# Positions instead of channels on the partitions for theta, and seven quadrant products for both pairs of batches

## The chip, the cores and the metric

One core of one Trainium2 chip. The metric is the device time of the whole program, in microseconds (us), the median of several runs.

## The reference, cut to what matters

Three layers follow each other, on four batches of 448 positions: attention (12 heads of 64), a gated MLP with spatial mixing ("moe"), and the layer that the change rewrites ("moe2"), in float32:

```python
def _moe2_ref(x, w_theta, w_tok_r, w_tok_i, w_ch):      # x: (4, 448, 768)
    theta = x @ w_theta                                  # w_theta: (768, 768)
    zr, zi = x * np.cos(theta), x * np.sin(theta)
    yr = np.einsum('ts,bsd->btd', w_tok_r, zr)           # w_tok_r, w_tok_i: (448, 448)
    yi = np.einsum('ts,bsd->btd', w_tok_i, zi)
    u = x + yr + yi
    return (u + np.maximum(u @ w_ch, 0.0)).astype(np.float32)   # w_ch: (768, 768)
```

Most weights arrive as 64-bit floats and are turned into 32-bit words on the chip.

## The kernel before, in words

**Precision.** A product of two float32 matrices is made of three matmuls in fp32r: both factors are split into a rounded part h and the rest l = x - h, and `three` gives h.h + h.l + l.h (L407). A split is one copy on ACT (h) and one subtraction on DVE or POOL (l, `difference`, L404).

**Layout.** From the first MoE on, an activation is held turned: `x2(b, m)` is a tile with 128 of the 768 channels on the partitions and the 448 positions in the columns; KD = 6 such blocks m for each of B = 4 batches b.

**The order of the work.** The program is a list of operations (`Plan.op`, L245): an engine, a due time, a cost, a function that issues the instructions, and keys that it reads and writes. The due times and costs don't run anything any more: `ORDER` (L47 to L217) is a permutation of all operations, written out as a list, and the instructions are issued in exactly that order, each engine's own in the order in which they stand there. Keys such as ("mm", 0) are buffers that are used in turn (`ring`).

**Theta and the mix (L1540 to L1676).** For each batch `split_x` (L1554) splits its six blocks. For each of the 24 blocks (b, m), `theta` (L1567) makes theta for 128 channels by 448 positions: 6 x 3 matmuls with the weights as the stationary factor and x as the moving one, 448 columns, into a bank "mm" (`th_ps`). Then come, on 448 columns each: `turns` on DVE (L1584, n = theta/2pi rounded by a magic number), `whole` on POOL (L1587), `rest_1`, `rest_2` and `clamp` on DVE (L1591 to L1599), in `second` `size` on DVE (L1603), `cosine` and `sine` on ACT (L1608 to L1612), and `real` and `imaginary` on DVE (L1616 to L1621), which multiply by x2. The result z (cos part and sin part side by side, 896 columns) has channels on the partitions. `mix` (L1633) needs positions there, since it sums over them: seven PE transposes of 128 x 128 turn z into a bank "s" (`z_ps`, L1651), ACT rounds all 896 columns (L1656), DVE subtracts (L1661, counted at L405), and 7 x 3 matmuls of 448 columns with the turned weights w_tok (`tok`) give y (`y_ps`), which DVE adds to x2 in place (L1673). The mix of a block stands two blocks behind its theta.

**Mixing weights.** `load_tok` (L1446) loads w_tok_r and w_tok_i, converts them, and `transpose_tok` (L1485) turns them in 7 steps kk of four PE transposes each (`tok_ps`, L1496), split into `tok_h` and `tok_l`.

**w_ch.** `load_w_ch` (L1682) loads it in 12 pieces of 128 x 384, converts and splits each at once into `ch_h` and `ch_l` (L405).

**Last product.** Batches 0 and 1 are done directly (L1713 to L1769): for each block 6 x 3 matmuls of 448 columns (`f_ps`), relu and sum on DVE, four PE transposes back (`o_ps`, L1751), copies and stores. Batches 2 and 3 are done together by `pair` (L1953): w_ch in four quadrants A11 to A22 and the two batches as a matrix of 2 x 2 blocks B, Winograd's form with seven products P1 to P7 in place of eight. Each product is 3 rows by 3 steps by 3 matmuls of 448 columns. `make_s` (L1859) makes the four sums S1 to S4 of quadrants, `begin` and `go_on` the sums T1 to T4 of the blocks of B, all of them split again; `plus` (L2026) adds products up in the parts `p`, `finish` (L2031) ends a block. The S parts lie in buffers of w_theta, the B parts in those of `tok` and of x's splits, the parts `p` and temporaries in those of z, zt and r.

Of the kernel before, what the change touches and what calls it, by code (L numbers as in the profile page):

```python
# [340 lines left out]
def attn_moe_moe2_kernel(ctx: ExitStack, tc: tile.TileContext, q, k, v, cap, w_in, w_sp, b_sp, w_out,  # L341
# [86 lines left out]
    def bank(over=True):  # L428
        turn[0] += over
        tag = ("mm", "av", "mm", "sum")[turn[0] % 4] if over else "mm"  # L430
        if tag == "mm":
            return ring("mm", 2), lambda: ps_mm.tile([128, 512], F32, tag="mm", name="ps_mm")
        return tag, lambda: ps_1.tile([128, 512], F32, tag=tag, name="ps_" + tag)

    def from_f64(t, bits, bits_key, hb, hb_key, wf, wf_key, to=None, to_key=None, early=1e9, engine="act"):


        n = {}
# [1339 lines left out]

# [423 lines left out]
```

## Time and profile before

| | |
|---|---|
| median of 3 runs (range) | 769.49 us (768.89 to 770.06) |
| the profiled execution: time / span | 769.43 us / 767.4 us |
| PE matmul / weight load busy | 752.9 us (98%) / 644.6 us (84%) |
| DVE / ACT / POOL busy | 603.4 (79%) / 453.3 (59%) / 300.0 us (39%) |
| instructions | 10971, of them 3732 matmuls |
| DMA | 59.26 MB, mean 77 GB/s |

The engines are PE (TensorE matmuls), PEld (its weight loads, which overlap), DVE (VectorE), ACT (ScalarE), POOL (GpSimd) and SP (which issues DMAs). A group's line of the profile gives the code line, the engine, the operation, output <- inputs by the program's names, the shape, the count, then busy us and the mean ns of one, then the idle time before them and what ended it. Matmuls overlap, so the mean of one is longer than the distance between two.

### The profile page before, as it was taken

Reading aid. Unit: us, or ns where it says so; the run is one execution under the profiler, and the core shown is the slowest. Engines: PE = TensorE matmul, PEld = TensorE weight load, DVE = VectorE, ACT = ScalarE, POOL = GpSimd, SP = SyncE. Lnnn points to the kernel's source line nnn. Section 1 sums busy time; section 2 is a strip of 40 time slices with the busy share of each in tenths; the row PEclk is TensorE's granted clock in tenths of the full one; section 3 lists DMA queues with packets and bytes.
Section 4 is the critical chain, followed back from the end, with each engine's and each line's share of the span. In section 5 each row is a group of like instructions: output and inputs, shape, how many; then the busy total and the mean of one; then the engine's idle time right before and its main releaser. Section 6 shows DMA issues by size and latency. Waiting matters only on the chain.

```text
span 767.4 us, 10971 instructions
## 1 busy us (share of the span) xinstructions
PE 752.9 (98%) x3732; PEld 644.6 (84%) x3732; DVE 603.4 (79%) x984; ACT 453.3 (59%) x752; POOL 300.0 (39%) x441
## 2 busy tenths in 40 slices
PE   8999899999999999999999999999999999999997
PEld 4665678888898888887899988999999999999986
DVE  4878978799677989889977766887778878757575
ACT  4999868787788788895565544423433333242333
POOL 4889587555445546651202001200201201437270
PEclk9999999999999999999999999999999999999999
DMA  6778333262333431412443410011010100000225
GB/s 175 202 195 211 79 86 95 60 132 56 79 98 71 117 87 42 119 37 61 125 145 102 144 46 1 21 30 33 21 42 21 41 21 1 2 1 0 73 77 139
DMA packets 78219, 59.26 MB, mean 77 GB/s; under 512 B 47074, under 2 KB 71364, under 8 KB 78164
## 3 DMA queue, kind: packets, MB, share of 16 engines
q1 hardware_dynamic: 76260, 54.61, 27.2%
q0 software_dynamic: 1152, 3.64, 1.5%
q8 instruction: 29, 0.48, 0.3%
q10 hardware_dynamic: 752, 0.33, 0.2%
q14 instruction: 26, 0.21, 0.1%
HBM read 44.18 MB, written 5.62 MB: 65 GB/s over the span
## 4 chain that ended last, share of the span: by engine, by line
PE 86%; DVE 5%; ACT 4%; POOL 2%; issue 2%; SPq 1%; DMA 0%; DVEq 0%; POOLq 0%; ACTq 0%
PE ps_mm L402 19%; PE y_ps L402 14%; PE acc L402 12%; PE th_ps L402 11%; PE f_ps L402 10%; PE sc L402 8%; PE ps_av L402 3%; PE ps_sum L402 3%; PE z_ps L1651 2%; PE tqk L709 2%; ACT e L819 1%; ACT e L822 1%; PE o_ps L1751 1%; DVE ll L405 1%; SPq L615 1%
## 5 line engine op out<-in xcount | busy, mean ns | idle before, releaser
L402 PE MATMUL y_ps<-tok_h,zt 128*128 128x448 f32 x336 | 104.6, 368 | 0.0
L1587 POOL TENSOR_SCALAR n<-n 128x448 f32<-128x448 f32 x24 | 15.0, 623 | 184.0 <-DVE n L1584 179.5
L822 ACT ACTIVATE e<-e,cap_sb 128x896 f32<-128x896 f32 x72 | 74.7, 1044 | 0.8
L819 ACT ACTIVATE e<-sc,icap 128x896 f32<-128x896 f32 x72 | 71.8, 1004 | 3.1 <-PE sc L402 2.3
L405 DVE TENSOR_TENSOR ll<-e,hh 128x896 fp32r<-128x896 f32 x54 | 62.8, 1167 | 8.3 <-ACT hh L827 4.8
L402 PEld LDWEIGHTS y_ps<-tok_h,zt 128*128 128x128 f32 x336 | 63.2, 188 | 6.1
L402 PE MATMUL y_ps<-tok_l,zt 128*128 128x448 f32 x168 | 62.0, 369 | 0.0
L1656 ACT CAST zt<-z_ps 128x896 fp32r<-128x896 f32 x24 | 21.8, 907 | 66.5 <-PE z_ps L1651 61.5
L402 PE MATMUL f_ps<-x,ch_h 128*128 128x448 f32 (+2 forms) x204 | 57.9, 365 | 0.7 <-DVE p L2028 0.5
L402 PE MATMUL th_ps<-x,th_ah 128*128 128x448 f32 x192 | 56.0, 373 | 0.2 <-DVE r L1591 0.2
L402 PE MATMUL ps_mm<-w_in_h,x 128*128 128x512 f32 (+1 forms) x132 | 47.4, 399 | 1.1 <-DVE w_sp_l L405 1.1
L402 PE MATMUL ps_mm<-x,w_in_h 128*128 128x448 f32 x168 | 48.4, 369 | 0.0
L405 POOL TENSOR_TENSOR x<-x,x 128x448 fp32r<-128x448 f32 x18 | 22.9, 1278 | 64.6 <-ACT x L1557 64.6
L402 PE MATMUL sc<-yl,XH 128*128 128x448 f32 x126 | 46.0, 365 | 0.0
L402 PE MATMUL acc<-ll,vh 128*128 128x448 f32 x108 | 40.4, 374 | 1.3 <-DVE ll L405 1.2
L405 DVE TENSOR_TENSOR zt<-z_ps,zt 128x896 fp32r<-128x896 f32 x24 | 26.2, 1091 | 18.9 <-ACT zt L1656 18.5
L402 PEld LDWEIGHTS f_ps<-x,ch_h 128*128 128x128 f32 x204 | 37.2, 188 | 4.4 <-DVE p L2028 0.9
L402 PE MATMUL acc<-hh,vh 128*128 128x448 f32 x108 | 39.5, 366 | 0.2 <-ACT xun L909 0.2
L402 PE MATMUL acc<-hh,vl 128*64 128x448 f32 x108 | 39.6, 367 | 0.0
L402 PEld LDWEIGHTS th_ps<-x,th_ah 128*128 128x128 f32 x192 | 35.0, 188 | 3.2 <-DVE r L1591 0.4
L402 PE MATMUL f_ps<-x,ch_l 128*128 128x448 f32 (+2 forms) x102 | 36.9, 362 | 0.0
L846 POOL TENSOR_SCALAR et_hl<-et 64x448 fp32r<-64x448 f32 x36 | 23.7, 658 | 32.3 <-ACT et L822 11.1
(306 smaller groups left out, 2244.4 us busy)
## 6 DMA issues: line engine op xcount, KB each, us to landing
y<-y SPq DMA_DIRECT2D x60, 112.0 KB, 2.3
bits<-in_moe_w_ch_dram SPq DMA_DIRECT2D x12, 384.0 KB, 3.1
rq<-in_q_dram SPq DMA_DIRECT2D x33, 128.0 KB, 3.1
rk<-in_k_dram SPq DMA_DIRECT2D x11, 384.0 KB, 4.2
r<-d SPq DMA_DIRECT2D x16, 224.0 KB, 3.8
rv<-in_v_dram SPq DMA_DIRECT2D x18, 192.0 KB, 2.7
w_in_bits<-in_moe_w_in_dram POOLq DMA_DIRECT2D x6, 512.0 KB, 5.3
w_in_bits<-in_moe_w_in_dram SPq DMA_DIRECT2D x6, 512.0 KB, 5.1
```

The lines of the kernel that those rows point to most:

```text
L402: nc.tensor.matmul(out=ps, lhsT=a, rhs=r, start=(first and i == 0), stop=(last and i == len(terms) - 1))
L405: (engine or nc.vector).tensor_tensor(out=o, in0=x, in1=f32(hi), op=ALU.subtract)
L615: queue.dma_start(out=twice()[0][hd][:, :, u], in_=q[b, h + hd, 0:384, :].rearrange("(r j) d -> r j d", j=3))
L709: nc.tensor.transpose(o, a, ident)
L819: nc.scalar.activation(out=st["e", g], in_=src, func=ACTF.Tanh, scale=icap)
L822: nc.scalar.activation(out=st["e", g], in_=st["e", g], func=ACTF.Exp, scale=cap_sb)
L846: nc.gpsimd.tensor_scalar(out=st["t", hd][r, :], in0=st["e", 0][r, :], scalar1=1.0, scalar2=0.0, op0=ALU.mult, op1=ALU.add)
L1587: nc.gpsimd.tensor_scalar(out=st["n"], in0=st["n"], scalar1=1.0, scalar2=-MAGIC, op0=ALU.mult, op1=ALU.add)
L1651: nc.tensor.transpose(st["t"][:, kk * 128:(kk + 1) * 128], z["z"][:, kk * 128:(kk + 1) * 128], ident)
L1656: nc.scalar.copy(out=st["h"].rearrange("p c n -> p (c n)"), in_=st["t"][:, 0:n])
L1751: nc.tensor.transpose(st["t"][0:w, i * 128:(i + 1) * 128], x2(b, m)[:, i * 128:i * 128 + w], ident)
```

## The change

Theta is made with positions on the partitions. Two batches' last 64 positions are put together into one tile of 128 (`split_tails`, tag xT), so a pair of batches has seven tiles of positions: four go with the even batch (three full ones and the shared tail), three with the odd one. The channels go in three units of 256. A unit has two halves d of 512 columns (two tiles of positions, or one in the odd batch's second half). x is the stationary factor, w_theta the moving one, with 256 columns. z comes out as the mix wants it, and is not turned; instead x is turned (fp32, into a bank "s", 10 or 6 transposes per unit), and `real` and `imaginary` multiply by it there. For the shared tail, cos and sin parts of one batch are placed on the two halves of the partitions, so `tok` gets an eighth step kk, with the two halves of w_tok exchanged. The first half of z is split by POOL, the second by DVE.

w_ch is converted but not split when it is loaded. Its quadrants are split before the first pair (`split_a`), into buffers of the tails, of the loads, of z and of zt; `make_s` adds whole numbers instead of h and l parts. `pair` runs for both pairs; the direct product is gone. `ORDER` is new throughout (3433 operations instead of 3395).

```diff
@@ transpose_tok
-        for kk in range(NC):
+        for kk in range(NC + 1):
             transpose_tok(t + 22.0 + 1.2 * kk, kk, slots)
...
-                nc.tensor.transpose(st["ps"][:, j * 128:j * 128 + n], ta[j // 2][0:n, j % 2, kk * 128:(kk + 1) * 128],
-                                    ident[0:n, 0:n])
+                if kk < NC:
+                    nc.tensor.transpose(o, a[:, kk * 128:(kk + 1) * 128], ident[0:n, 0:n])
+                    continue
+                nc.tensor.transpose(o, a[:, S - 128:S], ident[0:n, 0:n])
+                nc.tensor.transpose(o[LO], a[:, S:S + 64], ident[0:n, 0:n])
@@ split_tails (new): per batch of the pair
+        op("none", t - 1.0, 0.0, begin, r=["region"], w=[("xT", x, n) for x in "hl" for n in range(2)])
...
+            op("act", t, 0.5, lambda b=b: hi(b), r=rows, w=[("xT", "h", n)])
+            op("dve", t + 0.6, 0.5, lambda b=b: lo(b), r=rows + [("xT", "h", n)], w=[("xT", "l", n)], port=True)
@@ theta
-        t = chain(t, km, begin, [
-            (3 * C, lambda i=i: three(theta_w("h", i, m), theta_w("l", i, m), xs["h", i], xs["l", i]),
...
+        tiles = ((0, 1), (2, 3)) if even else ((0, 1), (2,))
...
+                    for k, m in enumerate(ms):
+                        o = st["x"][:, d * 512 + j * TW + k * 128:][:, 0:128]
+                        if p < 3:
+                            nc.tensor.transpose(o, x2(b, m)[:, p * 128:p * 128 + 128], ident)
+                        else:
+                            nc.tensor.transpose(o, x2(b + 1, m)[:, S - 128:S], ident)
+                            nc.tensor.transpose(o[LO], x2(b, m)[:, M:S], ident)
...
+                        for k in range(i, i + 2):
+                            xh, xl = positions(p, k)
+                            products(sd["ps"][:, j * TW:(j + 1) * TW], three(xh, xl, weights("h", k), weights("l", k)),
+                                     k == 0, k == KD - 1)
...
+            def hi(sd=sd, d=d, zd=zd, spans=spans):
+                st["H", d] = pools["wk"].tile([128, 4, TW], F32R, tag="H", name="zt", bufs=3)
...
+            e = "pool" if d == 0 else "dve"
...
+                ("act", 5.5, 0.9, hi, dict(r=[zr, zi, "region"], w=[zh])),
+                (e, 6.5, 2.1 if e == "pool" else 0.9, lambda lo=lo, e=e: lo(e=nc.gpsimd if e == "pool" else nc.vector),
+                 dict(r=[zr, zi, zh, "region"], w=[zl], port=True))] + [
+                ("act", 7.0, 0.35, tail_hi, dict(r=[zr, zi, "region"], w=[kth])),
+                ("dve", 7.4, 0.34, tail_lo, dict(r=[zr, zi, kth], w=[ktl], port=True))] * tail))
@@ mix
-                nc.tensor.transpose(st["t"][:, kk * 128:(kk + 1) * 128], z["z"][:, kk * 128:(kk + 1) * 128], ident)
...
-        op("pe", t, 0.77, transposes, r=z["zk"], w=[ks])
-        op("act", t + 0.9, 0.8, hi, r=[ks], w=["zth", "ztl"])
-        op("dve", t + 1.8, 1.0, lo, r=[ks, "zth"], w=["ztl"])
...
+            (3 * C, lambda i=i: three(z("H", i)[:, cols], z("L", i)[:, cols], tok["h", i // 4][:, i % 4, :],
+                                      tok["l", i // 4][:, i % 4, :]), keys(i) + [("tok", "h", i), ("tok", "l", i)])
+            for i in (0, 1, 4, 5, 2, 6, 3 if b % 2 == 0 else 7)])
@@ the loop over units: theta of unit i, mix of unit i - 1, then the split of unit i's second half
+    for i in range(B * N3 + 1):
...
+        if i >= 1:
+            b, c, z, keys = units[i - 1][:4]
+            for m in (2 * c, 2 * c + 1):
+                t = mix(b, m, z, keys, ("av", "sum")[n % 2], t)
...
+        if i < B * N3:
+            units[i][4]()
@@ the direct product of batches 0 and 1
-    for b in range(B - 2):
-        xs = split_x(b, t - 3.0)
...
-                (3 * C, lambda i=i, cols=cols, xs=xs: three(ch["h", i // 2][:, i % 2, cols], ch["l"][:, i, cols],
-                                                            xs["h", i], xs["l", i]),
...
@@ the quadrants' homes, their split, and make_s
+    HOMES = [("xT", None, 4), ("bits", None, 2), ("z", zs[0][1], 2), ("z", zs[1][1], 2), ("H", 0, 2)]
...
+    def split_a(q, i, t, e):
...
+        op("act", t, 0.42, lambda: nc.scalar.copy(out=a_of(q, i, "h"), in_=f32(w_of(q, i))), r=[kw], w=[kh])
+        op(e, t + 0.5, 0.47 if e == "dve" else 0.95, lambda: difference(
...
-        add(t, lambda: part(A21, "h"), lambda: part(A22, "h"), P, [key(A21, "h"), key(A22, "h")])
-        add(t + 0.1, a, lambda: part(A21, "l"), P, [kf, key(A21, "l")])
-        add(t + 0.2, a, lambda: part(A22, "l"), P, [kf, key(A22, "l")])
+        add(t, w(A21), w(A22), P, [w_key(A21, i), w_key(A22, i)])
         split(t + 0.3, 1)
...
@@ the end
-    t = pair(B - 2, t)
+    for c0 in range(0, B, 2):
+        t = pair(c0, t)
```

## Rows read from the trace of the kernel before

**Rows 1.** The clock of the core: us from first to last instruction, mean granted clock.
```profile
core 0: 767.4 us, clock 1.000
```
**Rows 2.** The page, part 1: busy us, share of the span, instructions.
```profile
PE 752.9 (98%) x3732; PEld 644.6 (84%) x3732; DVE 603.4 (79%) x984; ACT 453.3 (59%) x752; POOL 300.0 (39%) x441
```
**Rows 3.** Stages: length; PE, PEld, DVE, ACT, POOL busy; granted clock; DMA share; GB/s.
```profile
445.00:675.00 230.00, 229.79 (x1203) 209.46 (x1203) 176.09 (x322) 82.17 (x162) 39.10 (x46) 1.00 0.08 22
675.00:740.00 65.00, 64.90 (x341) 59.43 (x339) 42.86 (x72) 23.81 (x57) 31.54 (x26) 1.00 0.13 43
740.00:767.40 27.40, 22.00 (x132) 19.05 (x130) 17.00 (x30) 8.41 (x25) 5.05 (x5) 1.00 0.38 101
```
**Rows 4.** The page, part 4: the chain that ended last, by engine.
```profile
PE 86%; DVE 5%; ACT 4%; POOL 2%; issue 2%; SPq 1%; DMA 0%; DVEq 0%; POOLq 0%; ACTq 0%
```
**Rows 5.** Timeline of PE (start, us, what): theta matmuls, 24 from first row to last.
```profile
459.45 0.57 PE L402 MATMUL th_ps<-x,th_ah 128*128 128x448 f32 x2
...
464.32 0.69 PE L1496 MATMUL tok_ps<-ident,ta 128*128 128x128 f32 x4
```
**Rows 6.** Timeline of PE, the end: three matmuls of 256 columns, three of 192.
```profile
760.41 0.39 PE L402 MATMUL f_ps<-x,ch_h 128*128 128x256 f32 x2
...
760.76 0.37 PE L402 MATMUL f_ps<-x,ch_h 128*128 128x192 f32 x2
...
762.28 0.38 PE L402 MATMUL f_ps<-x,ch_h 128*128 128x192 f32 x2
...
762.61 0.39 PE L2097 MATMUL o_ps<-ident,x 128*128 128x128 f32 x2
```
**Rows 7.** Timeline of PE: seven transposes of z, three theta matmuls, the next ones.
```profile
564.54 0.93 PE L1651 MATMUL z_ps<-ident,z 128*128 128x128 f32 x7
565.22 0.65 PE L402 MATMUL th_ps<-x,th_ah 128*128 128x448 f32 x2
...
565.91 0.57 PE L402 MATMUL th_ps<-x,th_ah 128*128 128x448 f32 x2
```
**Rows 8.** Timeline of PE: two steps of turning the mixing weights, and the next matmul.
```profile
450.34 1.37 PE L1496 MATMUL tok_ps<-ident,ta 128*128 128x128 f32 x8
451.64 0.67 PE L402 MATMUL th_ps<-x,th_ah 128*128 128x448 f32 x2
```
**Rows 9.** Groups on DVE, whole span, shapes apart.
```profile
L405 DVE TENSOR_TENSOR zt<-z_ps,zt 128x896 fp32r<-128x896 f32 x24 | 26.2, 1091 | 18.9 <-ACT zt L1656 18.5
L1584 DVE TENSOR_SCALAR n<-th_ps 128x448 f32<-128x448 f32 x24 | 14.8, 618 | 3.3 <-PE th_ps L402 3.2
L405 DVE TENSOR_TENSOR ch_l<-wf,ch_h 128x384 fp32r<-128x384 f32 x12 | 6.5, 549 | 0.0
L2082 DVE TENSOR_TENSOR p<-f_ps,p 128x256 f32<-128x256 f32 x1 | 0.4, 424 | 0.1
```
**Rows 10.** Groups on POOL (445 to 675 us) and on ACT (400 to 767 us).
```profile
L405 POOL TENSOR_TENSOR x<-x,x 128x448 fp32r<-128x448 f32 x9 | 11.1, 1238 | 18.9 <-ACT x L1557 18.9
L1656 ACT CAST zt<-z_ps 128x896 fp32r<-128x896 f32 x24 | 21.8, 907 | 66.5 <-PE z_ps L1651 61.5 <-PE y_ps L402 5.0
```
**Rows 11.** Timeline of PE where theta starts; in brackets the idle time before.
```profile
466.13 0.68 PE L402 MATMUL th_ps<-x,th_ah 128*128 128x448 f32 x2 [0.21 <-DVE r L1591]
```
**Rows 12.** Timeline of PE, 740 us to the end: waits before products.
```profile
743.54 0.68 PE L402 MATMUL f_ps<-x,ch_h 128*128 128x448 f32 x2 [0.49 <-DVE p L2028]
...
746.89 1.48 PE L402 MATMUL f_ps<-x,S 128*128 128x448 f32 x6 [0.38 <-DVE p L2028]
...
758.54 0.88 PE L402 MATMUL f_ps<-x,S 128*128 128x448 f32 x3 [0.35 <-DVE p L2028]
```
**Rows 13.** Timelines of POOL and DVE: two subtractions that overlap.
```profile
668.51 1.02 POOL L1880 TENSOR_TENSOR S<-s_f,S 128x384 fp32r<-128x384 f32 x1 [4.12 <-ACT S L1876]
668.88 1.06 DVE L1880 TENSOR_TENSOR S<-s_f,S 128x384 fp32r<-128x384 f32 x1 [0.94 <-ACT S L1876]
```
**Rows 14.** Timeline of PE's weight loads in the last product.
```profile
697.03 0.19 PEld L402 LDWEIGHTS f_ps<-x,ch_l 128*128 128x128 f32 x1
```

More of the change, by code (lines that the diff above doesn't have):

```diff
@@ L459, in sign @@
             wu, top = wf().bitcast(U32), words()[:, :, 1]
-            ends = [(wu, top, wu)]
+            ends = [(wu if out is None else out().bitcast(U32), top, wu)]
             if to is not None:
@@ new lines, in attn_moe_moe2_kernel, with theta, transposes, weights @@
+    tl = {}
+    def theta(b, c, xs, t):
+        even = b % 2 == 0
+        ks = ring("s", 2)
+        ms = (2 * c, 2 * c + 1)
+        tiles = ((0, 1), (2, 3)) if even else ((0, 1), (2,))
+        st = {}
+        kth, ktl = [("tl", c, x) for x in "hl"]
+        def transposes():
+            st["x"] = ps_s.tile([128, 1024], F32, tag="s", name="x_ps")
+            for d in range(2):
+                for j, p in enumerate(tiles[d]):
+                    for k, m in enumerate(ms):
[5 more added lines that the diff above has]
+                            nc.tensor.transpose(o[LO], x2(b, m)[:, M:S], ident)
+        def weights(x, i):
+            return th[x, i][:, c * TW:(c + 1) * TW] if c < 2 else th[x, "b", i // 2][:, i % 2, :]
+        def positions(p, i):
+            if p < 3:
+                return xs["h", i][:, p * 128:p * 128 + 128], xs["l", i][:, p * 128:p * 128 + 128]
+            return xtail["x"][:, i, 0, :], xtail["x"][:, i, 1, :]
+        later = []
+        kd = []
+        for d in range(2):
+            stage("t%d" % d, b, c)
+            w = TW * len(tiles[d])
+            km, kn = ring("mm", 2), ring("vt", 3)
@@ new lines, in theta, with turns, whole @@
+            if d == 0:
+                op("pe", t, 0.109 * (10 if even else 6), transposes,
+                   r=[("x2", a, m) for a in ((b, b + 1) if even else (b,)) for m in ms], w=[ks])
+                t += 0.109 * (10 if even else 6)
+            def turns(sd=sd, w=w):
+                sd["n"] = keep.tile([128, w], F32, tag="vt", name="n", bufs=3)
+                nc.vector.tensor_scalar(out=sd["n"], in0=sd["ps"][:, 0:w], scalar1=INV_2PI, scalar2=MAGIC, op0=ALU.mult, op1=ALU.add)
+            def whole(sd=sd):
+                nc.gpsimd.tensor_scalar(out=sd["n"], in0=sd["n"], scalar1=1.0, scalar2=-MAGIC, op0=ALU.mult, op1=ALU.add)
@@ new lines, in tail_hi, with tail_lo @@
+            def tail_hi(sd=sd):
+                tl[c] = pools["wk"].tile([128, 2, TW], F32R, tag="tl%d" % c, name="zt_tail")
+                for o, a in tail_spans(sd, tl[c][:, 0]):
+                    nc.scalar.copy(out=o, in_=a)
+            def tail_lo(sd=sd):
+                for (o, a), (h, _) in zip(tail_spans(sd, tl[c][:, 1]), tail_spans(sd, tl[c][:, 0])):
+                    difference(o, a, h)
+            wide = w / 512
+            op("dve", t + 0.2, 0.6 * wide, turns, r=[km], w=[kn])
@@ new lines, in record, with rounded @@
+        def record(d, t_, ops_):
+            for e, dt, cost, f, kw in ops_:
+                op(e, t_ + dt, cost, f, **kw)
+        stage("z0", b, c)
+        record(*later[0])
+        stage("z1", b, c)
+        record(later[1][0], later[1][1], later[1][2][:5])
+        def rounded():
+            stage("zr", b, c)
+            record(later[1][0], later[1][1], later[1][2][5:])
+        where = {0: (0, 0), 1: (0, 1), 4: (0, 2), 5: (0, 3), 2: (1, 0), 6: (1, 2)}
+        where[3 if even else 7] = (1, 1) if even else None
@@ L1643, in mix, with z, keys @@
+        def z(x, i):
+            if where[i] is None:
+                return tl[c][:, "HL".index(x)]
+            return st[x, where[i][0]][:, where[i][1]]
+        def keys(i):
+            return [kth, ktl] if where[i] is None else kd[where[i][0]]
+        return b, c, z, keys, rounded, t
+    def mix(b, m, z, keys, bank, t):
         stage("m", b, m)
         st = {}
-        ks = ring("s", 2)
-        n = NC * 128
-        def transposes():
-            st["t"] = ps_s.tile([128, 1024], F32, tag="s", name="z_ps")
-            for kk in range(NC):
-                nc.tensor.transpose(st["t"][:, kk * 128:(kk + 1) * 128], z["z"][:, kk * 128:(kk + 1) * 128], ident)
@@ L1653, in hi @@
[L1653 to L1663 removed]
+        cols = slice(m % 2 * 128, m % 2 * 128 + 128)
@@ L1690, in load_w_ch, with load, hb @@
-        converted(t, w_ch[i * 128:(i + 1) * 128, c:c + CW], dst_h, lambda: ch["l"][:, i, c:c + CW], ("ch", i, c),
-                  pool="wk", bufs=1)
-    blocks = []
-    ch_loaded = []
-    WC, WD = (5, 3)
+        st = {}
+        kb, kh, kf = ring("bits", 1), "hb", ring("vt", 3)
+        def load():
+            st["b"] = pools["wk"].tile([128, CW], I64, tag="bits", name="bits", bufs=1)
+            nc.sync.dma_start(out=st["b"], in_=w_ch[i * 128:(i + 1) * 128, c:c + CW])
+        def hb():
+            if "s" not in st:
+                st["s"] = pools["wk"].tile([128, CW], F32, tag="hb", name="hb")
+            return st["s"]
@@ L1696, in attn_moe_moe2_kernel @@
+        op("sp", t - 6.0, 0.5, load, r=["region"], w=[kb], lag=3.0)
+        from_f64(t, lambda: st["b"], kb, hb, kh, wf, kf, to_key=ch_key(i, c), out=dst)
+    units = []
+    n_ch = 0
     t = u
     n = 0
-    for i in range(B * KD + 2):
-        if i < B * KD:
-            b, m = divmod(i, KD)
-            if m == 0:
-                xs = split_x(b, t - 3.0)
-            blocks.append(theta(b, m, xs, t))
-            t += 18 * C
-            if i == 0:
-                blocks[0][3](t + 3.0)
-            if i >= WC and (i - WC) % WD < 2 and len(ch_loaded) < 2 * KD:
-                j = len(ch_loaded)
-                ch_loaded.append(j)
-                load_w_ch(j // 2, j % 2 * CW, t)
-        if i >= 2:
-            b, m, z, _ = blocks[i - 2]
-            u = mix(b, m, z, ("av", "sum")[n % 2], t)
-            n += 1
-            if i - 1 < B * KD:
-                blocks[i - 1][3](t + 1.0)
-            t = u
@@ L1805, in open_parts @@
+    def open_parts(n):
         wk = pools["wk"]
[L1806 to L1814 removed]
```

448 lines of the change are left out of this document (248 added, 200 removed), and 340 rows, old and new, of the table ORDER.

## The prediction

> **What bounds the kernel now.** I read the clock first: TensorE is granted its full 2.4 GHz over the whole span, on the one core there is, so no term below is a matter of the clock [rows 1]. Then the engines: PE is busy 752.9 of 767.4 us, the next one, DVE, 79% of the span [rows 2]. A busy matmul queue need not be one that always has work waiting, so two more views. The table of stages shows how long PE was without work in the stretch that the change rewrites: 0.2 of the 230 us from the first theta block to the last mix, 0.1 of the next 65, and 5.4 of the last 27.4 [rows 3]. And 86% of the chain that ended last is PE [rows 4]. The reader should see that up to the last microseconds nothing but the length of PE's queue set the time there. So I count PE work first, and then ask whether the others can still feed it.
>
> One matmul's recorded duration is no price, because matmuls overlap. The price is the distance between starts: 24 theta matmuls of 448 columns without a break take 464.32 - 459.45 = 4.87 us, 0.203 each [rows 5].
>
> **The change on PE.** The sums are against the profiled execution, 769.43 us (its span of 767.4 and 2.0 around it), 0.06 us under the median of the three runs.
>
> Theta: 24 blocks of 18 matmuls of 448 columns become, per pair of batches, 7 tiles of positions by 3 units of 256 channels by 18, so 756 matmuls of 256. Both make 193,536 columns. Before: 432 x 0.203 = 87.7 us. The kernel has 256-column matmuls of this kind at its very end: three in a row take 760.76 - 760.41 = 0.35 us, 0.117 each [rows 6]; 756 x 0.117 = 88.2, so **+0.5 us**. From below: those of 192 columns take (762.61 - 762.28)/3 = 0.110 [rows 6], and 256 columns will not take less, so -4.5. From above: 0.203 us is 487 cycles, about one a column; less 192 columns at 2.4 GHz (0.080) it is 0.123, so +5.3. I take the row of the same shape, though it is only three matmuls long.
>
> Turning z: 24 visits of seven transposes go. A visit takes 565.22 - 564.54 = 0.68 us, 0.097 a transpose, and the three matmuls behind it need 0.69 where three need 0.61 elsewhere, so 0.08 more: 24 x 0.76 = 18.2 us [rows 5, 7]. Turning x comes in: a unit of an even batch has 6 full transposes and 2 pairs for the tails, 10, one of an odd batch 6; over 12 units that is 96 transposes in 12 visits, 96 x 0.097 + 12 x 0.08 = 10.3 us. Together **-7.9 us**. If the 24 in the tails' pairs cost as much as those of the mixing weights (next), 1.6 us comes back.
>
> Mixing weights: one more step of the loop over kk, with eight transposes instead of four. Eight take 451.64 - 450.34 = 1.30 us there [rows 8], **+1.4** with the switch; at the price of z it would be 0.9. The mix itself keeps 24 x 21 matmuls of 448 columns: nothing.
>
> Last product: the first two batches had 2 x 6 x 6 x 3 = 216 matmuls of 448 columns and get the 7 x 3 x 3 x 3 = 189 that the second pair has. 27 x 0.203 = **-5.5 us**. The 96 transposes of the output stay.
>
> PE's sum: +0.5 - 7.9 + 1.4 - 5.5 = **-11.5 us**, to 757.9.
>
> **What it asks of the others.** DVE: an operation takes 0.42 us at 256 columns and 0.62 at 448 [rows 9], so about 0.685 at 512. A pass over theta becomes 18 of 512 and 6 of 256, 14.9 us, where 24 of 448 took 14.8 [rows 9]: no change. The split of the turned z, 26.2 us [rows 9], becomes 6 x (0.685 + 4 x 0.42) + 6 x 0.685 = 18.3, since the first half of each unit goes to POOL. The split of w_ch, 6.5 us [rows 9], leaves this stage. In come the quadrants' own splits (six of 0.55 on DVE), the tails' (3 us) and the S sums, which must be ready for the first pair instead of the second (about 9 us). DVE goes from 176 of 230 us to about 178 of 219. POOL gets 12 subtractions of 1024 columns; one of 448 took 1.24 us [rows 10], so 2.8 each, 34 us on an engine busy 39 of 230 [rows 3]. ACT has 82 of 230 [rows 3] and keeps its columns. The copies and sums of a second pair stand beside 189 matmuls (38 us), as the first pair's did.
>
> All of that lies beside PE. The cover is what PE does between a unit's theta and its mix: two mixes (42 x 0.203 = 8.5 us) and the next unit's theta (7.0 or 9.5 with its transposes), 15.5 to 18. The chain under it: seven DVE operations (4.6 us), POOL's rounding (0.7), two sines (1.5), ACT's split (1.0, [rows 10]) and POOL's 2.8, in sum 10.6, with the queues' waits some 14. It fits, with little over.
>
> **Waits that it adds.** Where theta starts, PE has half a unit (4.2 us) to run before the buffers of the first MoE close, where it had two blocks; the second half needs the tails, whose copy and subtraction queue behind ACT's and DVE's last work for that MoE, and all later theta matmuls queue behind it on PE. The old kernel lost 0.21 us there [rows 11]. I take 0.5, between 0 and 3. Where theta ends, the direct products of two batches filled every gap. Now only P1 can (5.5 us): the pieces of A12 lie in the z and zt buffers and can be written only when the last unit is split, and P5 waits for S and T1. I take 0.5, between 0 and 4. The first pair brings the waits that the second has now, 0.49 + 0.38 + 0.35 = 1.2 us, all for DVE's sums [rows 12]. The end itself stays. With these 2.2 us: **760.1 us**.
>
> **The rivals.** *Seams*: the two places cost their upper ends, or the pitch is 0.123: 4 to 7 us more, 764 to 767. For it: the 0.2 us idle [rows 3] rests on filler that goes. Against: DVE has a fifth of its time free.
>
> *DVE and POOL in each other's way*, the one on the other side: a subtraction of 384 columns on DVE that ran beside one on POOL took 1.06 us [rows 13], where the same takes 0.55 alone [rows 9]. POOL's new 34 us could hold up as much of DVE's work: 178 + 34 = 212 of 219 us, with the chain's wait at the front of the units' mixes. It decides from 9.3/12 = 0.8 us a unit. If half of the 34 is not covered, 17 us: 777. Against it: many of DVE's operations here read PSUM, and the order of the work is written out.
>
> *Weight loads that stick out*: there are 324 more. If each stood in front of its matmul, at the 0.097 us that a transpose with its load takes [rows 7], that is 31 us: 791. The trace speaks against it: a load's own record is 0.19 us [rows 14], and yet matmuls of 448 columns, each with its load, start every 0.203 [rows 5]. The Trainium skill ("TensorE: Matmul & The Clock Gate", the section The mechanism, under row and column tiling) says that a load overlaps a running matmul only when it goes to another row group. By that rule this rival would hold; the trace disagrees with it, by the two numbers of the sentence before.
>
> *The change not doing what it says*: that 432 matmuls become 756 is plain in the diff, but the written-out order is new from its first entry, so attention and the first MoE may move by a microsecond or two either way. That lies in the range.
>
> **How the numbers follow.** Forecast, 755 to 764: 0.66. Below 755 (a pitch near 0.110, a better order): 0.05. Seams, 764 to 767.5: 0.15. All of the gain eaten, 768 to 771: 0.04. DVE and POOL: 0.08. Weight loads: 0.02. A measurement of this kernel tells 0.2% (1.5 us) from no change. So faster 0.86, same 0.04, slower 0.10. The range leaves out the slow cases, the even one and a little at the low end: 754.5 to 767.
>
> **What would show it.** Right: z_ps gone, and x_ps there with 96 transposes at 0.1 us; 756 theta matmuls starting 0.117 apart; 378 products of 448 columns in the last stage; PE without work for under 3 us from theta's start to the first S product. Wrong: theta matmuls 0.125 or more apart (the price of the narrow ones was misread); PE idle in front of y_ps in unit after unit, released by the zt split of POOL or DVE (the second rival); one hole of several us before the first S product (the seam); idle time in the attention stage, which would be the new order.

## The result, and the profile after

The changed kernel takes 762.97 us (median of four executions, 760.83 to 763.6) where the kernel before takes 769.62 (768.89 to 770.06): the ratio is 0.991, 95% interval 0.9888 to 0.9931. Timed again later, in six executions beside ten of the kernel before, it took 764.57 (760.25 to 765.85), ratio 0.9914 (0.989 to 0.9939). So it is faster, by 6.7 us in the first timing and 5.5 in the second, 0.9% each time; the forecast was 9.3 us. The profiled execution took 763.6 us with a span of 761.8.

Part 1 of the page after, against [rows 2]; then the table of stages (length; PE, PEld, DVE, ACT, POOL busy; granted clock; DMA share; GB/s), against [rows 3], whose last stage is now 5.6 us shorter:

```profile
PE 743.9 (98%) x3965; PEld 643.1 (84%) x3965; DVE 620.2 (81%) x992; ACT 476.0 (62%) x798; POOL 343.0 (45%) x464
```
```profile
445.00:675.00 230.00, 229.32 (x1486) 215.96 (x1485) 190.13 (x344) 102.06 (x202) 79.81 (x65) 1.00 0.08 25
675.00:740.00 65.00, 62.23 (x319) 55.06 (x318) 49.66 (x70) 28.25 (x67) 44.67 (x33) 1.00 0.15 40
740.00:761.80 21.80, 17.46 (x112) 15.36 (x110) 13.71 (x25) 8.66 (x26) 2.31 (x2) 0.98 0.52 138
```

PE still has work nearly all the time, but the middle line has changed: PE now stands still for 65.00 - 62.23 = 2.8 us where it stood still for 0.1. The timeline of PE (start, us, what, idle time before) shows the waits of the first pair of the last product:

```profile
669.75 1.49 PE L404 MATMUL f_ps<-x,a 128*128 128x448 f32 x6 [0.62 <-ACT p L2148]
...
681.76 1.49 PE L404 MATMUL f_ps<-x,S 128*128 128x448 f32 x6 [0.62 <-ACT p L2148]
...
699.65 0.88 PE L404 MATMUL f_ps<-x,a 128*128 128x448 f32 x3 [0.72 <-DVE p L2152]
...
701.85 2.74 PE L404 MATMUL f_ps<-x,S 128*128 128x448 f32 x12 [0.72 <-DVE p L2152]
...
712.12 2.11 PE L404 MATMUL f_ps<-x,a 128*128 128x448 f32 x9 [0.71 <-DVE p L2152]
```

Theta, in the same view: six matmuls of 256 columns on the tails, then thirty on x, to the next mix; behind them twenty transposes of x, to the next theta matmul:

```profile
478.54 0.28 PE L404 MATMUL th_ps<-th_ah,x_tails 128*128 128x256 f32 x1
...
479.24 0.28 PE L404 MATMUL th_ps<-th_bh,x 128*128 128x256 f32 x1
...
482.83 0.36 PE L404 MATMUL y_ps<-tok_h,zt 128*128 128x448 f32 x1
...
483.44 0.81 PE L1624 MATMUL x_ps<-ident,x 128*128 128x128 f32 x6
...
485.54 0.37 PE L404 MATMUL th_ps<-th_bh,x 128*128 128x256 f32 x1
```

That is 0.70/6 = 0.117 us a matmul on the tails, 3.59/30 = 0.120 on x, 2.10/20 = 0.105 a transpose.

For the whole account I took, in both traces, the distance from the start of each PE instruction to the start of the next and summed it by the tile that it writes (so idle time counts with what stands before it). The sums make up the spans:

| PE's time, us | before | after | difference | forecast |
|---|---|---|---|---|
| attention and first MoE | 449.88 | 451.33 | +1.5 | 0 |
| theta | 90.00 | 90.62 | +0.6 | +0.5, and 0.5 of waits |
| turning z, or x | 17.03 | 9.90 | -7.1 | -7.9 |
| turning the mixing weights | 4.53 | 5.53 | +1.0 | +1.4 |
| mixes | 103.91 | 104.16 | +0.2 | 0 |
| last product and its output transposes | 97.34 | 95.58 | -1.8 | -5.5, and 1.7 of waits |
| before PE's first start, and after its last | 4.72 | 4.69 | 0 | 0 |
| span | 767.4 | 761.8 | -5.6 | -9.3 |

Two lines are off: the last product gave 2.0 us less than forecast, and the early stages, which compute the same as before, took 1.5 more. The experiments go to these first.

### The profile page after: what moved, and what is told of

It reads as the page before. It is cut to its first block, busy times and chain, and to the rows that moved or that the text cites. A ratio compares the mean times of both kernels' runs of the same rounds, so it can differ in the third digit from the quotient of the medians.

```text
span 761.8 us, 11555 instructions
## 1 busy us (share of the span) xinstructions
PE 743.9 (98%) x3965; PEld 643.1 (84%) x3965; DVE 620.2 (81%) x992; ACT 476.0 (62%) x798; POOL 343.0 (45%) x464
## 4 chain that ended last, share of the span: by engine, by line
PE 72%; DVE 5%; ACT 2%; POOL 1%; issue 1%; DVEq 0%; POOLq 0%; ACTq 0%
PE ps_mm L404 16%; PE y_ps L404 12%; PE th_ps L404 12%; PE f_ps L404 10%; PE acc L404 7%; PE sc L404 5%; PE ps_sum L404 3%; PE ps_av L404 3%; PE o_ps L2172 1%; PE tqk L711 1%; PE x_ps L1624 1%; DVE ll L407 1%; DVE p L2152 1%; DVE s L995 1%; PE tok_ps L1500 1%
## 5 line engine op out<-in xcount | busy, mean ns | idle before, releaser
L404 PE MATMUL th_ps<-th_ah,x 128*128 128x256 f32 x288 | 57.4, 284 | 0.0
L407 POOL TENSOR_TENSOR zt<-z,zt 128x1024 fp32r<-128x1024 f32 x12 | 29.6, 2470 | 59.2 <-ACT zt L1739 59.2
L407 POOL TENSOR_TENSOR x<-x,x 128x384 fp32r<-128x384 f32 (+1 forms) x15 | 18.5, 1242 | 74.0 <-ACT x L1565 65.1
L404 PE MATMUL f_ps<-x,S 128*128 128x448 f32 x216 | 49.8, 372 | 1.6 <-DVE p L2152 1.0
L404 PEld LDWEIGHTS th_ps<-th_ah,x 128*128 128x128 f32 x288 | 46.8, 190 | 0.8
L404 PEld LDWEIGHTS f_ps<-x,S 128*128 128x128 f32 x216 | 39.6, 188 | 6.3 <-DVE p L2152 1.6
L404 PE MATMUL f_ps<-x,a 128*128 128x448 f32 (+2 forms) x171 | 38.8, 362 | 2.3 <-DVE p L2152 1.7
L1739 ACT CAST zt<-z 128x1024 fp32r<-128x1024 f32 (+2 forms) x36 | 24.3, 691 | 26.2 <-DVE z L1710 22.7
L404 PE MATMUL th_ps<-th_al,x 128*128 128x256 f32 x144 | 40.6, 282 | 0.0
L450 ACT ACTIVATE hb<-bits 128x384 f32<-128x384 f32 (+4 forms) x40 | 22.7, 567 | 27.6 <-DMA bits<-in_moe_w_ch_dram 15.5
```

The costliest lines, as they stand in the source:

```text
L404: nc.tensor.matmul(out=ps, lhsT=a, rhs=r, start=(first and i == 0), stop=(last and i == len(terms) - 1))
L407: (engine or nc.vector).tensor_tensor(out=o, in0=x, in1=f32(hi), op=ALU.subtract)
L450: nc.scalar.activation(out=hb(), in_=f32(words()[:, :, 1]), func=ACTF.Copy, scale=2.0 ** -112)
L1739: nc.scalar.copy(out=o, in_=a)
```

## The experiments

Single executions of one kernel lie some microseconds apart here, so I read each run's account of PE's time beside its median.

**Where the last product loses.** The five waits have one thing in common in the written-out order. The banks of this product are, but for two, halves of tiles of 1,024 PSUM columns (`ps_s`). Take the first wait, with PE and ACT side by side (timelines):

```profile
664.01 1.40 PE L404 MATMUL f_ps<-x,a 128*128 128x448 f32 x6
...
667.73 1.40 PE L404 MATMUL f_ps<-x,a 128*128 128x448 f32 x6
```
```profile
669.16 0.53 ACT L2148 COPY p<-f_ps 128x448 f32<-128x448 f32 x1 [0.88 <-PE f_ps L404]
```

ACT's copy reads P1 of row block 2, whose last matmuls are among the six at 664.01. ACT is free for it from 668.28 on, but waits for PE until 669.13, where the matmuls of 667.73 end: the last three of them are P2, and write the *other* half of the same tile. PE's next P2 matmuls write that half again, and wait for the copy (669.69) until 669.75. So the order holds a round trip, PE to ACT to PE, between two matmuls that neither reads nor writes what is copied. The other four waits have the same pattern. DVE's three sums among them are not late either: DVE stands idle ahead of each, until PE is done (timeline of DVE):

```profile
698.97 1.16 DVE L2152 TENSOR_TENSOR p<-f_ps,p 128x448 f32<-128x448 f32 x2 [0.96 <-PE f_ps L404]
...
701.17 0.62 DVE L2152 TENSOR_TENSOR p<-f_ps,p 128x448 f32<-128x448 f32 x1 [1.04 <-PE f_ps L404]
...
711.44 0.62 DVE L2152 TENSOR_TENSOR p<-f_ps,p 128x448 f32<-128x448 f32 x1 [0.65 <-PE f_ps L404]
```

In the written-out order of the whole last product, five reads of a half stand directly between two operations of PE on the other half, with nothing else of PE's between, and they are these five. Nine reads in the first pair are of the two banks that are tiles of their own; two of them also stand directly between two steps on one other bank, and PE waits for none of the nine. After each of the five, the next product starts 0.99 to 1.08 us after the last, where 0.206 is usual, and the one behind it after 0.31: 4.2 + 0.5 = 4.7 us for all five.

Edit, named *halves*: the five copies and sums are issued elsewhere. In each pair of numbers the first operation goes behind the second: 3080 is the copy of P1 r=2 (2956 opens its buffer), 3116 the copy of P5 r=2, 3158 the sum of P7 r=0, 3196 and 3226 the sums of P4 r=1 and 2, 3101 and 3102 a finished block and its transposes, 3271 a matmul step of the second pair.

```diff
+for a, b in [(2956, 3076), (3080, 2956), (3116, 3142), (3101, 3157), (3102, 3195), (3158, 3157), (3196, 3203), (3271, 3267), (3226, 3263)]:
+    ORDER.remove(a)
+    ORDER.insert(ORDER.index(b) + 1, a)
```

> Theory (two halves of one PSUM tile wait for each other): in the first pair of the changed kernel PE stands still five times, each time where the copy or sum of one half of a 1024-column PSUM tile is issued between two products of the other half; the next product then starts 0.99 to 1.08 us after the last instead of 0.206, and the one behind it 0.10 later than usual, in sum 4.7 us. With those five copies and sums issued elsewhere (and two neighbours moved to make room) the five waits are gone: 3.5 to 4.7 us less, 758.3 to 759.5 against 762.97. Rival (DVE and POOL in each other's way make the sums late): the waits come back at other places of the first pair, the time stays within 1 us of 763.

Measured: none of the five is left at its place, but two other waits have come up (timeline of PE, all waits from 664 to 716 us; then one sum in the timeline of DVE):

```profile
698.50 2.08 PE L408 MATMUL f_ps<-x,a 128*128 128x448 f32 x9 [0.81 <-DVE p L2156]
705.14 0.88 PE L408 MATMUL f_ps<-x,a 128*128 128x448 f32 x3 [1.08 <-DVE p L2156]
```
```profile
702.87 0.62 DVE L2156 TENSOR_TENSOR p<-f_ps,p 128x448 f32<-128x448 f32 x1 [1.85 <-PE f_ps L408]
```

The edit made the wait of 1.08 us itself: this is the moved sum of P4 r=1, which holds DVE's queue for 1.85 us until PE is done, and the sum that PE then needs stands behind it. Ahead of the wait of 0.81 us DVE didn't wait for PE; it is late itself there (see *best*).

PE's time for the last product falls from 95.58 to 93.60 us. The median stays at 762.9 (757.93 to 764.55, ratio 0.9897, 0.9871 to 0.9923). The profiled execution's early stages took 453.21 us, 1.9 more than in the changed kernel's profile; the two executions at a clock of 1.000 took 757.93 and 758.58 us, the four at 0.994 to 0.996 took 762.4 to 764.55. Half a hit: the gain is 2.0 in the stage where I expected 3.5 to 4.7, and the median doesn't show it. Waits at other places of the pair are also what the rival said, so this run alone doesn't decide between the two.

The counter-test, *p1_twice*, puts 27 matmuls back ahead of the waits:

```diff
                     b2 = slot(sl[B][i])
+                    for _ in range(3 if name == "P1" and c0 == 0 and i == 0 else 0):
+                        products(bank_of(kb)[:, 0:n], three(ah, al, b2[:, 0, cols], b2[:, 1, cols]), True, True)
```

> 27 matmuls of 448 columns put back in: the first three products of each P1 chain of the first pair are made four times (each restarts the sum, so the result is the same). Theory (the waits of the first pair are round trips between two halves of one tile): more time before them doesn't cure them, the full 27 x 0.206 = 5.6 us come back, and the five waits stay at 0.6 to 0.7 us each; 768.5. Rival (the waits are DVE being late): the extra 5.6 us let DVE catch up, the waits shrink by half or more, and only 2 to 4 us come back: 765 to 767.

Measured: 769.74 us (765.21 to 771.08), ratio 1.0002 (0.9986 to 1.0018): the change's whole gain is used up. The last product takes 100.87 us, 5.3 more. And with 5 us more time ahead of them the waits are what they were (timeline of PE, all waits from 664 to 716 us):

```profile
671.30 1.51 PE L404 MATMUL f_ps<-x,a 128*128 128x448 f32 x6 [0.62 <-ACT p L2150]
683.33 1.49 PE L404 MATMUL f_ps<-x,S 128*128 128x448 f32 x6 [0.62 <-ACT p L2150]
701.23 0.87 PE L404 MATMUL f_ps<-x,a 128*128 128x448 f32 x3 [0.72 <-DVE p L2154]
703.43 2.74 PE L404 MATMUL f_ps<-x,S 128*128 128x448 f32 x12 [0.72 <-DVE p L2154]
713.70 2.47 PE L404 MATMUL f_ps<-x,a 128*128 128x448 f32 x11 [0.72 <-DVE p L2154]
```

A late DVE would have caught up. With DVE's idle time ahead of its sums, this settles the round trips as the cause of the five, and the price of the 27 matmuls, 5.3 us.

*halves2* goes for the wait of 1.08 us with one more pair in the list, `(3179, 3166)`, the sum of P3 r=1.

> As in the first run of its kind, and the sum of P3 of the second row block (P3, r = 1) put ahead of the sum that now waits on PE. Theory: of the two waits that were left in the first pair there, the one of 1.08 us was made by the moved sum, which holds DVE's queue for 1.85 us until PE is done; it goes, and 0.8 to 1.2 us with it, so that the matmuls and transposes of the last product take 92.4 to 92.8 us of PE's time (95.6 in the changed kernel, 93.6 in the first run). The wait of 0.81 us stays, since there DVE is late itself: its subtractions take 1.5 us beside POOL's. Rival: both are DVE being late; the wait of 1.08 stays or moves on.

Measured: that wait is gone, 0.81 stays, and a new one of 1.06 us has come up in the second pair, for a copy that stands in ACT's queue behind two casts which wait for POOL. PE's time for the last product is 93.81: nothing gained on the run before. The median is 759.99 (758.01 to 761.77), ratio 0.9885 (0.9865 to 0.9906). My forecast for the wait held, the one for the stage did not.

**Is PE what sets the time of the theta stage?** *x_twice* makes 72 of the 96 transposes of x twice:

```diff
-                            nc.tensor.transpose(o, x2(b, m)[:, p * 128:p * 128 + 128], ident)
+                            for _ in range(2):
+                                nc.tensor.transpose(o, x2(b, m)[:, p * 128:p * 128 + 128], ident)
```

> 72 of the 96 transposes of x are made twice, into the same place. Theory (PE's queue sets the time of the theta stage and a transpose has its price of 0.104 us between starts): 72 x 0.104 = 7.5 us more, 770.5, and no idle time of PE between 445 and 665 us. Rival (DVE, busy 190 of 230 us there, sets the pace and a longer PE only fills its slack): 3 us more or less than that.

Measured: 769.58 us (768.04 to 771.23), ratio 1.0006 (0.9996 to 1.0017). PE's time for the transposes grows from 9.90 to 17.76, 7.9/72 = 0.109 each, and PE is never idle (stage table):

```profile
445.00:665.00 220.00, 220.00 (x1476) 208.74 (x1475) 172.19 (x326) 91.17 (x177) 66.01 (x53) 1.00 0.09 25
```

*lo_dve* takes the 12 long subtractions from POOL again:

```diff
-            e = "pool" if d == 0 else "dve"
+            e = "dve"
```

> The 12 subtractions of 1024 columns that the change gives to POOL (29.6 us there) made on DVE instead. By 0.62 us for 448 columns they cost DVE 12 x 1.4 = 17 us. Theory (PE sets the pace, DVE and POOL do get in each other's way but all of it is covered): the time stays within 1 us of 763, and DVE's busy time in the theta stage rises by clearly less than 17 us, since what it lost beside POOL comes back. Rival (DVE is what the stage hangs on): PE waits in front of the mixes, 2 us or more.

Measured: 763.33 us (762.58 to 764.21), ratio 0.9925 (0.991 to 0.994), the same as with POOL. First the changed kernel: the stage from 445 to 665 us, a group on DVE in it, and the group on POOL (page):

```profile
445.00:665.00 220.00, 219.94 (x1441) 207.75 (x1440) 180.89 (x333) 96.24 (x189) 72.28 (x59) 1.00 0.09 26
```
```profile
L407 DVE TENSOR_TENSOR x<-x,x 128x384 fp32r<-128x384 f32 x6 | 7.4, 1243 | 0.0
```
```profile
L407 POOL TENSOR_TENSOR zt<-z,zt 128x1024 fp32r<-128x1024 f32 x12 | 29.6, 2470 | 59.2 <-ACT zt L1739 59.2
```

Then this run, the stage and two groups on DVE:

```profile
445.00:665.00 220.00, 220.00 (x1443) 207.97 (x1442) 187.78 (x345) 96.39 (x189) 44.75 (x49) 1.00 0.09 25
```
```profile
L407 DVE TENSOR_TENSOR zt<-z,zt 128x1024 fp32r<-128x1024 f32 x12 | 14.8, 1234 | 2.2 <-ACT zt L1739 2.1
...
L407 DVE TENSOR_TENSOR x<-x,x 128x384 fp32r<-128x384 f32 x6 | 3.2, 548 | 0.0
```

DVE takes on 14.8 us and is busy only 187.78 - 180.89 = 6.9 more; the other 7.9 it had lost beside POOL. The 1243 ns are a mean of six: three ran beside a subtraction of POOL's and took 1.36 to 2.77 us, the other three 0.54 to 0.55. The longest, with POOL's beside it, in the changed kernel (timelines of DVE and POOL):

```profile
503.36 2.77 DVE L407 TENSOR_TENSOR x<-x,x 128x384 fp32r<-128x384 f32 x1
```
```profile
503.13 2.58 POOL L407 TENSOR_TENSOR zt<-z,zt 128x1024 fp32r<-128x1024 f32 x1 [1.53 <-ACT zt L1739]
```

PE notices none of it.

**The early stages.** In the profile after, the granted clock was at its lower level, 0.50 (1.2 GHz), from 82 to 85 us, behind 4 us in which PE had work for 2.66 (stage table):

```profile
78.00:82.00 4.00, 2.66 (x12) 1.28 (x11) 3.89 (x7) 3.39 (x7) 2.54 (x4) 0.98 0.59 153
82.00:85.00 3.00, 3.00 (x9) 2.56 (x9) 2.94 (x5) 1.30 (x3) 0.15 (x1) 0.50 0.36 89
```

By the share of each slice (0.93 from 81 to 82, 0.86 from 85 to 86) 0.07 + 1.5 + 0.14 = 1.7 us are lost by my estimate, about what the early stages are longer; matmuls of 512 columns start 0.42 us apart in that stretch and 0.23 behind it. Four runs ask whether that is the cause. *bias_later* closes PE's gaps at the transposes of w_sp; operation 375, the bias, goes behind the third split of w_sp:

```diff
+for a, b in [(375, 388)]:
+    ORDER.remove(a)
+    ORDER.insert(ORDER.index(b) + 1, a)
...
-        op("dve", t - 0.5, 1.2, bias, r=[kb], w=["spl"])
+        op("dve", t - 0.5, 1.2, bias, r=[kb], w=["splb"])
```

> Theory: TensorE's granted clock fell to 0.50 between 82 and 85 us of the changed kernel's profile because PE had gaps of 0.55, 0.56 and 0.23 us just before, at the transposes of w_sp, which wait for DVE; with 1.9 us of DVE work (the bias) moved behind the split that frees the bank, the first two gaps close, the granted clock stays at 1.00, and 1.1 (the gaps) to 3.0 us (gaps and 1.9 us of half speed) go: 760 to 762 against 762.97. Rival: the clock falls there whatever the gaps are: at most 1.1 us less, and a stretch of 0.50 is still in the profile.

Measured: 762.93 us (760.05 to 763.74), ratio 0.9904 (0.9887 to 0.9921). In the profiled execution (760.05) the clock is 1.00 up to 757 us and the early stages take 448.01; but PE now waits 1.6 us for ACT a little later, and of the other five executions four took 762.83 to 763.74 at a mean clock of 0.996 to 0.998. Not confirmed.

*early_old*, with the order of the kernel before for the first 1,800 operations:

```diff
+ORDER = OLD[:1800] + [i for i in ORDER if i not in set(OLD[:1800])]
```

> The first 1,800 operations (attention and most of the first MoE) in the written-out order of the kernel before, the rest as changed. Theory: the new early order alone costs the 1.5 us by which the first MoE ends later in the profile of the changed kernel (1.3 us more idle time on PE before 445 us and 1.9 us of half clock, less what other waits gave back): 1 to 2 us less, 761 to 762 against 762.97, and a granted clock of 1.00 throughout. Rival: the early stages of the two kernels differ by chance from run to run: no change beyond 0.5 us.

Measured: 762.62 us (761.63 to 763.33), ratio 0.9912 (0.9897 to 0.9927), and a clock of 0.999 or 1.000 in all four executions. The early stages take 448.55 us, 2.8 less than in the profile after; the last product takes 96.72, with a sixth wait. The clock came out as expected, but the median moved by 0.35 us only, within the 0.5 of the rival.

*after_again*, the changed kernel once more:

> The changed kernel as it is, beside the one before it in this list and timed as often. Its time was 760.83 once at a granted clock of 1.000 and 762.68 to 763.6 at 0.996 to 0.999. If the fallen clock is what parts these, executions of 1.000 stay near 761 and the others near 763; if it is chance of other kinds (when the first loads land, say), clock and time don't go together. Median expected 761 to 763.3; PE's time for the last product 95.6 us again, whatever the clock.

Measured: 764.57 us (760.25 to 765.85), above the 761 to 763.3 I expected. Its profile has the lower clock at another place, the start, behind a first wait of 2.0 us for the first part of q (stage table):

```profile
0.00:8.00 8.00, 4.85 (x13) 1.76 (x14) 2.49 (x11) 1.28 (x1) 3.68 (x14) 1.00 0.55 134
...
9.00:12.00 3.00, 3.00 (x10) 1.50 (x11) 1.95 (x4) 1.48 (x3) 0.92 (x3) 0.50 0.43 97
```

Clock and time go together only loosely: 760.87 us at 0.996, 765.1 at 0.997. The last product took 96.77 here, not 95.6: the sixth wait again.

*old_start*, where the first 100 entries come from the order before, so that q is loaded first:

```diff
+ORDER = OLD[:100] + [i for i in ORDER if i not in set(OLD[:100])]
```

> The first 100 entries of the written-out order from the kernel before, the rest as changed. In the profile of the kernel before the first transposes of q follow the warm-up matmuls at 5.84 us without a wait and the first score matmul starts at 11.16; as changed the first part of q is loaded behind two others, the transposes wait 1.56 (1.97 in the second profile), the scores start at 12.34 (12.99), and in three profiles of that start the granted clock was 0.50 for 3.41 us from 8.4 to 8.9 us on. Theory: with the old start the wait is 0.8 us or less, the scores start near 11.2, the clock is 1.00 up to 80 us, and the executions lie closer together: 759.5 to 762.5, median 761 or a little below, where the changed kernel had 760.25 to 765.85. Rival: the spread comes from the dip at 82 us alone: times from 760 to 764, as before.

Measured: 763.88 us (760.99 to 765.45), ratio 0.9921 (0.9901 to 0.9942). The profile does what I expected (the first transposes follow at 5.82 us without a wait, the clock is 1.00, early stages 449.08), the executions don't: 765.19 us came at a clock of 1.000. The theory falls as the cause of the spread, and the rival, the dip alone, with it.

All profiles together say more than these four runs. In the thirteen after the change, theta and the mixes keep their times within 0.5 us; it is the early stages that differ, from 447.8 to 453.3 us. The five profiles with a stretch of the lower clock ahead of 445 us took 451.3 or more there, the eight without one 450.7 or less. So the clock goes with the longer times, and something else spreads either group by 2 to 3 us. And the eight profiles with the changed kernel's own early order took 447.8 to 453.2 us: the one of the kernel before, with 449.88, lies among them, so these runs don't show the 1.5 us of the table to be a price of the new order.

**A difference in pitch.** *align* asks why theta on x runs at 0.120 and on the tails at 0.117:

```diff
-            st["h", i], st["l", i] = x[:, 0, 0:M], x[:, 1, 0:M]
+            x = x.rearrange("p a n -> p (a n)")
+            st["h", i], st["l", i] = x[:, 0:M], x[:, M:2 * M]
```

> The low part of x put right behind its high part (384 columns further, not 448). Theory A: the theta matmuls on x start 0.120 us apart and those on the tails 0.117 because the low part of x lies at an odd place; with the new place they fall to 0.117: 648 x 0.003 = 1.9 us less, 761.0. Theory B: the place of the stationary operand has no price, and the difference comes from the moving one or from the order: no change within 0.5 us, pitch still 0.120.

Measured: theta on x takes 77.88 us in both kernels, to the hundredth. Theory B; that the median of 760.9 us (760.04 to 763.17), ratio 0.9893 (0.9877 to 0.991), meets theory A's 761.0 is chance, since no theta matmul became faster.

**All together.** *best* has the moves of halves2, `(3312, 3272), (3313, 3312), (3249, 3313)` for the wait in the second pair (two casts and a subtraction go behind the copy), and the bias; *best2* has the old start besides.

> Together: the moved copies and sums of the second run of that kind, the copy of P1's third row block in the second pair put ahead of two casts that wait for POOL (a wait of 1.06 us had come up there), and the bias behind the splits of w_sp. Theory: the last product takes 92.3 to 93.0 us of PE's time (95.6 as changed), only the wait of 0.8 us for DVE is left in the two pairs ahead of the end, and the first MoE ends 1 us earlier; 757.5 to 759.5 in executions of full clock. Rival: what is taken from one wait comes up in the next, since DVE is 0.9 busy there: 93.8 or more.

> All of it: the old start, the bias moved, the copies and sums moved. Theory: each takes its own part, 1.5 us at the start, 1 at the transposes of w_sp, 2.5 in the last product: 757 to 759.5 in most executions, and below 759 in the median. Rival: DVE or the loads take back what the start gives, as an earlier PE waits at the next place: 760 or more.

Measured: *best* 761.99 us (760.57 to 763.1), ratio 0.9887 (0.987 to 0.9904); *best2* 761.04 (760.25 to 761.43), ratio 0.9887 (0.9869 to 0.9904). The last product takes 93.10 and 93.35 us of PE's time; the one wait left in the first pair of *best* is for DVE, which didn't wait for PE ahead of it; two of its operations of 384 columns between 691 and 697 us take 1.5 where 0.55 is usual [rows 9], beside POOL (timelines of PE, DVE, POOL):

```profile
698.59 2.10 PE L408 MATMUL f_ps<-x,a 128*128 128x448 f32 x9 [0.82 <-DVE p L2156]
```
```profile
691.69 1.49 DVE L2005 TENSOR_TENSOR s_f<-ch 128x384 f32<-128x384 f32 x1
...
695.43 1.51 DVE L411 TENSOR_TENSOR a<-ch,a 128x384 fp32r<-128x384 f32 x1
696.86 1.67 DVE L2156 TENSOR_TENSOR p<-f_ps,p 128x448 f32<-128x448 f32 x3
```
```profile
691.24 2.96 POOL L411 TENSOR_TENSOR x<-t_f,x 128x448 fp32r<-128x448 f32 x2
...
695.32 2.62 POOL L2271 TENSOR_TENSOR p<-p 128x448 f32<-128x448 f32 x2
```

In the stage the gain over the changed kernel is 2.2 to 2.5 us, and it is clear of chance: the last product took 95.2 to 96.8 us in the eight profiles without the moves and without added matmuls there, 93.1 to 93.8 in the four with them. The forecasts of the total failed: the two executions of *best* at a clock of 1.000 took 760.57 and 762.61 us where I expected 757.5 to 759.5, and the median of *best2* lies on its rival's side. In the total the three kernels with the moves of halves2 have ratios of 0.9885 to 0.9887 and the changed one 0.991 and 0.9914; their intervals overlap, so the total alone doesn't prove it. The early stages took 453.33 and 451.47 in these two profiles, with the lower clock at the start in the one and from 86 us on in the other, behind the wait of 1.6 us that moving the bias had uncovered.

## Why the prediction was right, and where it missed

The side and the range held; 760.1 was 2.9 us too low by the first timing, 4.5 by the second. That one, 764.57, lies where the forecast put the seams, but not for that reason: from 445 us to the first wait of the last product, at 669 us, PE stands idle 0.06 us in all. The steps in turn.

*Theta, +0.5*: right by its difference, +0.6. Both levels were too low, by 2.3 and 2.4 us, and that the two errors cancel is luck, since their causes differ: 0.203 [rows 5] is a stretch without a switch, and over all 432 matmuls the mean is 90.00/432 = 0.208; the narrow ones cost 0.120 on x, and the 0.117 of the three at the end [rows 6] only on the tails. A row of the same shape was the right one to choose, and the bounds 0.110 and 0.123 hold.

*Turning, -7.9*: -7.1. The 96 transposes cost 9.90 where I had 10.3; the z that went was worth 17.0, not 18.2. x_twice shows the price sticks out in full.

*Mixing weights, +1.4*: +1.0, near the bound of 0.9.

*Last product, -5.5 and waits of 0.5 + 1.2*: the matmuls were priced right (p1_twice: 5.3 for the same 27), **the waits were the step that failed**. "The first pair brings the waits that the second has now ... all for DVE's sums" took over the size of [rows 12] and its cause. The first pair has five round trips worth 4.7 us where the sum had 1.7 for these waits; the second pair and the end, which were to stay, gave 1.0 back (waits over 0.1 us there sum to 1.1 us, before to 2.1). That is the 2.0 by which the line falls short. The cause of the five is neither DVE's load nor POOL's, but where the order puts a read of one half of a tile. The clue stood in the profile of before: the three waits of [rows 12] are of the same kind, only shorter. By the order of that kernel the sums that PE waits for there (P6 r=1, P3 r=1, P3 r=2) read one half of a tile, and the matmul that waits is the second step of another product (P4 r=0, P7 r=1, P7 r=2) on the other half, which needs nothing else of that sum. So the kind of wait was taken over rightly; its number and size hang on the order, and the new order stands in the changed kernel's `ORDER`. Going through it for reads of one half directly between two steps on the other shows just the five, before any run.

*Where theta starts, 0.5*: no idle time at all. Against the forecast of 3.8 us for the last product and of 0.5 at the start, the sum of the misses is 2.0 + 1.5 (early) + 0.8 (turning) + 0.2 (mixes) + 0.1 - 0.4 - 0.5 = 3.7. Between 760.1 and the profiled 763.6 there are 3.5 us; the other 0.2 lies outside the span, which has 2.0 us around it before and 1.8 after.

*The order new from its first entry, a microsecond or two either way*: +1.5 us in the profile, so within what was said. Whether the new order costs anything stays open: eight profiles with it spread over 5.4 us. The lower clock accounts for 1.7 us in the profile of after by the estimate above; four runs could not tie the spread of the executions to it alone.

*DVE and POOL in each other's way*: it happens, 7.9 us of DVE's time in the theta stage, as lo_dve shows, and it costs PE nothing there; the cover was long enough. The Trainium skill ("SBUF — State Buffer", the section SBUF: two separate sides) says that a DVE instruction with two inputs in SBUF and a GpSimd instruction that reads SBUF share a pair of ports, that whichever starts first holds it for its whole instruction and the other waits. The trace agrees: the subtraction that began at 503.36, inside POOL's of 503.13 to 505.71, ended 0.42 us after it, and alone it takes 0.55. Only in the first pair does it seem to reach PE, with the 0.8 us that are left in *best*; no run took POOL's work away there, so that stays argued from the timelines.

*Weight loads that stick out*: they don't. There are 756 in theta, each by its record 0.190 us long, longer than the 0.120 from matmul to matmul; so this trace too speaks against the rule of the Trainium skill ("TensorE: Matmul & The Clock Gate", the section The mechanism) that the prediction weighed. The two forms of the largest group on the tile (ns: minimum, median, maximum):

```profile
L404 PEld LDWEIGHTS th_ps<-th_ah,x x288: 186/190/193, 449.2 to 628.5; 128*128 128x128 f32 x144
L404 PE MATMUL th_ps<-th_ah,x x288: 277/283/386, 449.4 to 628.6; 128*128 128x256 f32 x144
```

*What would show it right*: 96 transposes at 0.1 us, 756 matmuls at 0.117 to 0.120, 0.7 us of idle PE up to the first S product were all there, and so were the 378 products, nine of them cut into 256 and 192 columns; "one hole of several us before the first S product" was not. Of the five waits the first, 0.62 us, stands ahead of that product, the others behind it.

## What to carry to other kernels

When a sum of PE work is right and the time still falls short, look for waits of one size that repeat: 0.62 and 0.72 us, five times, is a round trip, not a load, above all if the engine that is waited for stood idle itself. If more time ahead of a wait doesn't shorten it, look at what it is that is waited for; here two halves of one PSUM tile, which the program treats as one, and what counts is where the copy or sum is issued: ACT's and DVE's waited alike. Moving them got back 2.0 to 2.5 of the 4.7 us, since a moved sum can make a wait of its own. And price each side of an exchange from a row of its own shape and its own operands: here two levels were wrong for different reasons, and the right difference was luck.

## What was not expected of the hardware

The lower granted clock turns up in short stretches at different places from execution to execution (in the changed kernel's two profiles from 82 us on and from 9 us on, in *best2* from 86), each time behind a stretch where PE had been waiting, though an equal wait need not have that effect: with the transposes of q waiting 1.9 us the profile of *align* has 1.000. The executions of the changed kernel spread over 5.6 us (760.25 to 765.85, ten of them) where 53 of the kernel before, timed beside the runs here, lie within 4.3 (767.81 to 772.08). The clock explains a part at most, and the spread of the profiles lies in the early stages; what else makes it is open. So is why theta on x runs at 0.120 and on the tails at 0.117.
